# Exponent words one slot pair earlier and a later value-rest copy, in a fused attention and mixture-of-experts kernel on one Trainium2 core

## Chip, cores and metric

The kernel runs on one core of a Trainium2 chip. The metric is device time in microseconds (us) of one execution; three timed runs of the kernel before gave 1537.13, 1540.23 and 1555.36 us, median 1540.23 us. Engines are named as the profile names them: PE is TensorE (PEld its weight loads), DVE is VectorE, ACT is ScalarE, POOL is GpSimd, SP is SyncE, which issues most DMAs.

## What is computed

The reference is pooled-key attention, a dense two-layer block with a leaky ReLU, and a top-1 mixture of eight experts:

```python
k_p = k.reshape(B, H, Sp, 8, D).mean(axis=3)          # B=8, H=8, S=576, D=64, Sp=72
v_p = v.reshape(B, H, Sp, 8, D).mean(axis=3)
attn = softmax(q @ k_p.T / sqrt(D))
x = (attn @ v_p).transpose(0, 2, 1, 3).reshape(4608, 512)
h = x @ w_in                                           # 512 x 2048, float64 in HBM
y = np.maximum(0.01 * h, h) @ w_out                    # 2048 x 512, float64 in HBM
e = argmax(y @ w_gate); g = softmax(y @ w_gate)[e]     # 8 experts
out = g * (np.maximum(y @ w1[e], 0) @ w2[e])           # 512 x 1024 x 512, float64 in HBM
```

The three weight matrices and the activations are multiplied as pairs of float32 parts (high and rest), three products for each.

## The kernel before

**Slots.** The 4608 tokens are 18 blocks of 256 tokens. For each block the dense layer runs over 16 slices f of the 2048 hidden units. One step (block b, slice f) is a slot. Slots 0 to 3 are (0, 0) to (0, 3). From slot 4 to slot 26 the first two blocks alternate: even slots are (0, f), odd slots (1, f - 4). An even slot and the odd one behind it are called a pair here. Slots 27 to 31 finish block 1, and from slot 32 on the blocks follow each other, 16 slots each. The order is written out by hand: each engine gets its instructions in the order in which the loop (the list `seq`, and `at(slot, function)` for work hung on a slot) records them, and works them off in that order.

**What a slot does.** `g1` (L498) makes 12 matmuls of 256 columns into a PSUM bank. ACT copies 0.01 of it (L131, `g<-h`), DVE takes the maximum (L506, `g<-g,h`), ACT rounds it to the high part (L131, `ghl<-g`, function `g_hi`), and in the next slot DVE subtracts that from it for the rest (L134, `ghl<-g,ghl`, function `g_lo`). `g2` (L526) makes 6 matmuls of 512 columns of the slot two before. Two PSUM banks take turns for `g1`.

**Weight conversion.** In slots 0 to 25 the two dense weights of a slice, 128 x 1024 float64 numbers in all, are turned into float32 pairs. `w_load64` (L450, L451) loads both halves into one of three buffers `raw`. `w_conv1a` first lets ACT make the exponent words (L463, absolute value of the top 16 bits into `ab_t`; L464, a Relu with scale and bias that shifts and rebiases into `e_t`), then lets DVE put in the sign (L465, on `e_t`) and shift the high mantissa (L468). `w_conv1b` puts in the low mantissa bits (L474) and joins exponent and mantissa (L477). `w_conv2` lets ACT round to the high part (L131, `w<-raw`) and DVE subtract (L134, `w<-raw,w`). There is one `e_t` and one `ab_t`. The function `conv` hangs this on the slots: in the even slot of a pair with slice f stand `w_conv2(0, f + 1)` and `w_conv1a(f + 2)`, in the odd slot `w_conv2(1, f + 1)`, `w_load64(f + 4)` and `w_conv1b(f + 2)`; in slots 0 to 3 all of it stands in one slot.

**Keys and values of the second batch.** They are loaded unpooled into the places of later weights and pooled by matmuls with a band matrix: `kvn_k` at slots 6, 8, 10 and 12 (L254), `kvn_v` at slot 14 (L269, then ACT and DVE in turn write `vm`, L275), `kvn_r` at slot 16: a product (L282), a masked copy by DVE into the tile that held the values (L284), and `v_rest` (four ACT copies into `vr` and two DVE subtractions, all through helpers at L131 and L134).

**Further on.** Block 0's routing uses transposes of its output (`y_tr`, slots 31 and 32), a small product (`y_logit`, slot 33), `route_a` (slot 34) and `route_b` and `route_c` (slots 36, 38). From slot 34 on the expert weights are split and stored. `final` makes the step list of the experts out of small tiles at the end of the dense part; behind it come the experts' steps.

Of the kernel before, what the change touches and what calls it, by code (L numbers as in the profile page):

```python
# [21 lines left out]
def kernel(  # L22
# [89 lines left out]
    second = []  # L112

    def sb(shape, dt, tag, bufs=1):
        return (second[0] if tag in ("ps", "kv", "y4", "junk") else pool).tile(shape, dt, name=tag, tag=tag, bufs=bufs)
# [163 lines left out]
    def kvn_r(nb):  # L279
        t = kvn[1]  # L280
        p = pt("att")
        nc.tensor.matmul(p[0:64], rep8.rearrange("p a b -> p (a b)"), t[0:64, 4], start=True, stop=True)  # L282
        f = t[0:64, 0].rearrange("p (h d) -> p h d", h=H)
        nc.vector.scalar_tensor_tensor(  # L284
            out=f, in0=p[0:64].rearrange("p (h d) -> p h d", h=H), scalar=float(POOL),
            in1=mask8.unsqueeze(2).to_broadcast([64, H, D]), op0=ALU.mult, op1=ALU.mult,
        )
        v_rest(nb % 2, f)
# [171 lines left out]
    def w_conv1a(f, kinds=BOTH):  # L460
        _, hw, e, ab = words(f, kinds)
        h = raw[f % 3][:, kinds].bitcast(BF16).rearrange("p k (n t) -> p (k n) t", t=4)[:, :, 3]
        nc.scalar.activation(ab, h, AF.Abs)  # L463
        nc.scalar.activation(e, ab.bitcast(U16), AF.Relu, scale=8.0 * 65536.0, bias=ebias)  # L464
        nc.vector.scalar_tensor_tensor(  # L465
            out=e, in0=hw, scalar=0x80000000, in1=e, op0=ALU.bitwise_and, op1=ALU.bitwise_or
        )
        nc.vector.tensor_scalar(  # L468
            out=hw, in0=hw, scalar1=3, scalar2=0x7FFFF8, op0=ALU.logical_shift_left, op1=ALU.bitwise_and
        )  # L470
# [204 lines left out]

    def final(c):
        V = nc.vector
        n = sb([P, E], F32, "fn")
        ni = sb([P, E], I32, "fni")
# [8 lines left out]
        m, m2 = sb(sq, F32, "g", 2), sb(sq, F32, "g", 2)  # L688
        key, pp, u, r = [sb([P, E], F32, "f" + x) for x in ("k", "q", "u", "w")]
        V.scalar_tensor_tensor(out=key, in0=n, scalar=float(E), in1=rank0, op0=ALU.mult, op1=ALU.add)  # L690
        pre, end = sb([P, E], F32, "fp"), sb([P, E], F32, "fe")
        ft = sb([P, 4], F32, "ft")
        tot, row, tv = ft[:, 0:1], ft[:, 1:2], ft[:, 2:3]
        cv = sb([P, 2], F32, "fcv")
# [33 lines left out]
        ri = sb([P, 1], I32, "fri")  # L728
# [3 lines left out]
    def final_list(cv):  # L732
# [6 lines left out]
        er, ch = etab[0:1], sb([1, NSS], F32, "fch")  # L739
# [273 lines left out]
    def plan():  # L1013
# [95 lines left out]
    with tc.manual_schedule():  # L1109
# [5 lines left out]
        e_t = start.tile([P, 1024], U32, name="e_t")  # L1115
# [35 lines left out]
        att_c(0)  # L1151
        w_conv1a(0, slice(0, 1))
# [5 lines left out]
        w_conv2(0, 0)  # L1158
        w_conv1a(0, slice(1, 2))
# [23 lines left out]
        def conv(s, b, f):  # L1183
# [17 lines left out]
        for s, (b, f) in enumerate(seq):  # L1201
# [171 lines left out]
```

## Time and profile before

| | us |
|---|---|
| timed runs | 1537.13, 1540.23, 1555.36 |
| the profiled execution's own time | 1544.75 |
| its span (first to last instruction) | 1542.8 |
| PE busy | 1471.1 |
| DVE busy | 930.8 |
| ACT busy | 618.3 |
| POOL busy | 336.7 |

The span is what the profile's times count from. Busy time leaves out waits. In a timeline row the numbers are start and duration; the bracket behind a row is the idle time of its engine just before, and what ended it. A wait is put down to the releaser that came last. Matmuls are pipelined and their ends are modelled, so a busy PE is not a PE at its peak.

### The profile page before, as it was taken

The page shows a single profiled execution, that of the slowest core. Times are in us where ns is not written, and L with a number is a line of the kernel's source. Part 1 is how long each engine was busy: PE and PEld are TensorE (multiplying, and loading weights), DVE is VectorE, ACT ScalarE, POOL GpSimd, SP SyncE. Part 2 cuts the span into 40 slices and gives each one's busy share as a digit, 9 for nine tenths or more (in the row PEclk, how much of TensorE's full clock was granted, in tenths as well). Part 3 has the DMA queues.
Part 4 walks back from the last instruction along what each step waited for, and adds up shares of the span by engine and source line. Part 5 has one row for each costly group of instructions (what it writes and reads, how often), then busy time and mean ns, then how long its engine had stood idle before and what let it go on. Part 6 is the DMA issues. An engine that isn't in the chain of part 4 may idle for free. (4 is left out here: it accounts for less than half of the span.)

```text
span 1542.8 us, 25661 instructions
## 1 busy us (share of the span) xinstructions
PE 1471.1 (95%) x9272; PEld 1314.5 (85%) x9272; DVE 930.8 (60%) x2387; ACT 618.3 (40%) x1412; POOL 336.7 (22%) x318
## 2 busy tenths in 40 slices
PE   3688999999999999999999999999999999999998
PEld 3575889899898888899989989988899999988886
DVE  6988768888778878877887977774212112111111
ACT  4565534545444454444444444322222222212222
POOL 4000212232232233223222232111121212111111
PEclk8699999999999999999999999999999999999999
DMA  9533145465544545545645634133611118566160
GB/s 214 149 121 117 60 139 166 157 207 174 158 168 166 182 146 187 179 146 167 192 168 154 209 137 164 62 138 138 266 55 48 49 35 324 200 251 261 42 256 19
DMA packets 121385, 238.05 MB, mean 154 GB/s; under 512 B 56845, under 2 KB 65041, under 8 KB 117544
## 3 DMA queue, kind: packets, MB, share of 16 engines
q1 hardware_dynamic: 90312, 139.81, 29.0%
q10 hardware_dynamic: 23328, 76.56, 13.4%
q0 software_dynamic: 7616, 20.01, 3.9%
q8 instruction: 75, 1.23, 0.3%
q14 instruction: 54, 0.44, 0.1%
HBM read 317.78 MB, written 87.38 MB: 263 GB/s over the span
## 5 line engine op out<-in xcount | busy, mean ns | idle before, releaser
L526 PE MATMUL y<-w,ghl 128*128 128x512 f32 x1728 | 466.5, 406 | 3.9 <-DVE ghl L134 3.1
L526 PEld LDWEIGHTS y<-w,ghl 128*128 128x128 f32 x1728 | 309.0, 191 | 64.1 <-DVE ghl L134 9.5
L134 POOL TENSOR_TENSOR ps<-ps 128x512 f32<-128x512 f32 x128 | 181.6, 1418 | 466.1 <-ACT ps L131 395.1
L498 PEld LDWEIGHTS h<-x_t,w 128*128 128x128 f32 x1776 | 238.9, 194 | 36.3 <-DVE w L134 14.7
L498 PE MATMUL h<-x_t,w 128*128 128x256 f32 x1776 | 246.3, 288 | 19.9 <-DVE w L134 12.8
L546 DVE CUSTOM_DVE_ANT_0 junk<-y,wg 128x512 bf16<-128x512 f32 x256 | 201.9, 789 | 1.9
L498 PEld LDWEIGHTS y<-x_t,w 128*128 128x128 f32 x1488 | 193.2, 189 | 9.6
L498 PE MATMUL y<-x_t,w 128*128 128x256 f32 x1488 | 196.2, 282 | 0.0
L938 PE MATMUL y<-w,ghl 128*128 128x512 f32 x672 | 175.4, 399 | 0.9 <-DVE ghl L926 0.9
L938 PEld LDWEIGHTS y<-w,ghl 128*128 128x128 f32 x672 | 119.7, 189 | 22.3 <-DVE ghl L926 1.3
L994 POOL DMA_INDIRECT out_dram<-kv,sidx x40 | 40.2, 1006 | 372.7 <-ACT kv L993 188.0
L131 ACT ACTIVATE g<-h 128x256 f32<-128x256 f32 x164 | 62.8, 383 | 141.3 <-PE h L498 129.1
L926 DVE SCALAR_TENSOR_TENSOR ghl<-h,ghl 128x256 fp32r<-128x256 f32 x56 | 23.8, 425 | 136.1 <-ACT ghl L925 136.1
L506 DVE TENSOR_TENSOR h<-g,h 128x256 f32<-128x256 f32 x132 | 56.0, 425 | 74.3 <-ACT g L131 73.9
L134 DVE TENSOR_TENSOR at_t<-a,at_t 128x512 fp32r<-128x512 f32 x62 | 42.7, 689 | 87.1 <-ACT at_t L131 86.8
L131 ACT ACTIVATE ps<-ps 128x512 fp32r<-128x512 f32 x128 | 80.5, 629 | 20.1 <-DMA ps<-in_moe_w_dram 13.1
L131 ACT ACTIVATE ghl<-h 128x256 fp32r<-128x256 f32 x132 | 50.5, 382 | 91.6 <-PE y L526 43.1
L131 ACT ACTIVATE ghl<-y 128x256 fp32r<-128x256 f32 x124 | 47.2, 380 | 95.2 <-DVE y L506 52.0
L131 ACT ACTIVATE g<-y 128x256 f32<-128x256 f32 x124 | 47.3, 382 | 61.0 <-PE y L498 54.2
L613 POOL DMA_INDIRECT lst<-ent,six x36 | 37.4, 1039 | 152.7 <-DVE six L612 112.7
L297 DVE TENSOR_TENSOR kv<-kv 72x512 f32<-72x512 f32 (+8 forms) x126 | 68.5, 544 | 3.2
L134 DVE TENSOR_TENSOR ghl<-h,ghl 128x256 fp32r<-128x256 f32 x132 | 55.5, 421 | 24.3 <-ACT ghl L131 23.9
(272 smaller groups left out, 2131.3 us busy)
## 6 DMA issues: line engine op xcount, KB each, us to landing
w<-wsp SPq DMA_DIRECT2D x108, 2048.0 KB
wsp<-ps ACTq DMA_DIRECT2D x128, 512.0 KB
ps<-in_moe_w_dram SPq DMA_DIRECT2D x128, 256.0 KB
y_d<-y ACTq DMA_DIRECT2D x18, 512.0 KB
raw<-in_moe_w_in_dram SPq DMA_DIRECT2D x16, 512.0 KB
raw<-in_moe_w_out_dram SPq DMA_DIRECT2D x16, 512.0 KB
q<-in_q_dram SPq DMA_DIRECT2D x28, 256.0 KB
kv<-in_k_dram SPq DMA_DIRECT2D x24, 288.0 KB
```

The lines of the kernel that those rows point to most:

```text
L131: nc.scalar.activation(o, i, AF.Copy, scale=scale)
L134: eng.tensor_tensor(out=o, in0=a, in1=b, op=ALU.subtract)
L297: eng.tensor_tensor(out=o, in0=t[:, :, 0:w], in1=t[:, :, w:2 * w], op=ALU.add)
L498: nc.tensor.matmul(p[:, 0:BLK], win(f)[:, kk, l], xv[:, kk, r], start=(n == 0), stop=(n == 3 * KD - 1))
L506: nc.vector.tensor_tensor(out=g, in0=t, in1=h, op=ALU.max)
L526: nc.tensor.matmul(y_ps[b, i], hl[:, l, i * P:i * P + P], wout(f)[:, r], start=(f == 0 and l + r == 0), stop=(last and l == 1),)
L546: nc.vector.tensor_tensor_reduce(out=jk, in0=y_sb[b][:, i], in1=wg_t[0][:, e], scale=1.0, scalar=0.0, op0=ALU.mult, op1=ALU.add, accum_out ...
L613: nc.gpsimd.indirect_dma_start(out=lst, out_offset=bass.IndirectOffsetOnAxis(ap=ix[:, 0:1], axis=0), in_=ent[:, i, :], in_offset=None, bou ...
L926: nc.vector.scalar_tensor_tensor(out=hl[:, 1], in0=b, scalar=0.0, in1=f32(hl[:, 0]), op0=ALU.max, op1=ALU.subtract)
L938: nc.tensor.matmul(o_ps[2 * p + i], hl[:, l, i * P:i * P + P], w[:, r], start=(f == 0 and l + r == 0), stop=(f == 7 and l == 1),)
L994: nc.gpsimd.indirect_dma_start(out=out, out_offset=bass.IndirectOffsetOnAxis(ap=sidx[:, t:t + 1], axis=0), in_=o, in_offset=None, bounds_c ...
```

## The change

`w_conv1a` loses its two ACT instructions to a new function `w_exp`. There are two exponent tiles, used in turn. `w_exp` of a slice is issued at the end of the odd slot's conversion (behind `w_conv1b(f + 2)`, for slice f + 3); in slots 0 to 3 likewise, and for slices 1 and 2 before slot 0. `v_rest` of the second batch leaves `kvn_r` (slot 16) and is hung on slot 18. Small tiles of the routing move to a pool that is opened after slot 31, block 0's routing is hung on later slots, and `final` takes its scratch from the gate weights' tile.

```diff
+    THIRD = ("junk", "rtmp", "roh", "cnt", "ent", "etmp", "rmx", "six", "erow", "eri")
...
-        return (second[0] if tag in ("ps", "kv", "y4", "junk") else pool).tile(shape, dt, name=tag, tag=tag, bufs=bufs)
+        return (second[0] if tag in ("ps", "kv", "y4") else second[1] if tag in THIRD else pool).tile(shape, dt, name=tag, tag=tag, bufs=bufs)
...
@@ kvn_r
-        v_rest(nb % 2, f)
...
@@ words
-        return rw[:, :, 0], rw[:, :, 1], e_t[:, 0:n], ab_t[:, 0:n]
+        return rw[:, :, 0], rw[:, :, 1], e_t[f % 2][:, 0:n], ab_t[:, 0:n]
...
-    def w_conv1a(f, kinds=BOTH):
-        _, hw, e, ab = words(f, kinds)
+    def w_exp(f, kinds=BOTH):
+        _, _, e, ab = words(f, kinds)
         h = raw[f % 3][:, kinds].bitcast(BF16).rearrange("p k (n t) -> p (k n) t", t=4)[:, :, 3]
         nc.scalar.activation(ab, h, AF.Abs)
         nc.scalar.activation(e, ab.bitcast(U16), AF.Relu, scale=8.0 * 65536.0, bias=ebias)
+
+    def w_conv1a(f, kinds=BOTH):
+        _, hw, e, _ = words(f, kinds)
         nc.vector.scalar_tensor_tensor(
...
@@ final: every sb(...) tile becomes spare(...), a slice of the gate weights' tile
-        n = sb([P, E], F32, "fn")
-        ni = sb([P, E], I32, "fni")
+        n = spare([P, E])
+        ni = spare([P, E], I32)
...
@@ plan, block 0
                 at(30, y_evac, 0)
-                at(31, y_tr, 0, 0)
-                at(32, y_tr, 0, 1)
-                at(33, y_logit, 0)
-                r = (34, 36)
+                at(33, y_tr, 0, 0)
+                at(35, y_tr, 0, 1)
+                at(36, y_logit, 0)
+                r = (37, 39)
...
-        e_t = start.tile([P, 1024], U32, name="e_t")
+        e_t = [start.tile([P, 1024], U32, name=f"e{i}") for i in range(2)]
...
@@ before slot 0
+        w_exp(0, slice(0, 1))
         w_conv1a(0, slice(0, 1))
...
+        w_exp(0, slice(1, 2))
         w_conv1a(0, slice(1, 2))
...
+        w_exp(1)
         w_conv1a(1)
         w_conv1b(1)
+        w_exp(2)
...
         at(16, kvn_r, 1)
+        at(18, v_rest, 1, kvn[1][0:64, 0].rearrange("p (h d) -> p h d", h=H))
...
@@ conv
                 if alone or b == 1:
                     w_conv1b(f + 2)
+                    if f + 3 < NF:
+                        w_exp(f + 3)
...
@@ after slot 31
                 stack.close()
+                second.append(ctx.enter_context(tc.tile_pool(name="third", bufs=1, side="right")))
```

On ACT, one pair of slots before the change (slots 8 and 9; `w_551` and `w_554` are places of converted weights, `raw_112` is the slice whose exponent words are made, `kT` belongs to `kvn_k`):

```order
L131 ACTIVATE w_551<-raw_111 128x4x128
L463 ACTIVATE ab_t<-raw_112 128x1024
L464 ACTIVATE e_t<-ab_t,ebias 128x1024
L131 ACTIVATE ghl<-g 128x256
L131 ACTIVATE g<-h_765 128x256
L131 ACTIVATE w_554<-raw_111 128x512
L131 ACTIVATE ghl<-g 128x256
L131 ACTIVATE g<-h_796 128x256
L131 ACTIVATE kT_71<-a_813 64x72 x2
L131 ACTIVATE w_827<-raw_112 128x4x128
```

The exponent words stand in the even slot, between that slot's rounding of `w_551` and its `ghl<-g`. The same pair after the change:

```order
L132 ACTIVATE w_554<-raw_112 128x4x128
L132 ACTIVATE ghl<-g 128x256
L132 ACTIVATE g<-h_766 128x256
L132 ACTIVATE w_557<-raw_112 128x512
L463 ACTIVATE ab_t<-raw_111 128x1024
L464 ACTIVATE e_109<-ab_t,ebias 128x1024
L132 ACTIVATE ghl<-g 128x256
L132 ACTIVATE g<-h_799 128x256
L132 ACTIVATE kT_71<-a_816 64x72 x2
L132 ACTIVATE w_830<-raw_113 128x4x128
```

They have moved into the odd slot, ahead of that slot's `ghl<-g` and of the next even slot's `g<-h`, and they are of the slice after the one that DVE has in hand.

On DVE, slot 16 before the change (`w_342` is the tile with the second batch's values, `vr_75` their rest):

```order
L506 TENSOR_TENSOR g<-g,h_1009 128x256
L134 TENSOR_TENSOR ghl<-g,ghl 128x256
L284 SCALAR_TENSOR_TENSOR w_342<-a_1026,mask_79 64x512
L134 TENSOR_TENSOR vr_75<-w_342,vr_75 32x256 x2
L134 TENSOR_TENSOR w_827<-raw_112,w_827 128x4x128
L465 SCALAR_TENSOR_TENSOR e_t<-raw_110,e_t 128x1024
```

And DVE in slot 18 after it, where the two `vr` subtractions now stand, ahead of the softmax of a token tile (`st`, `pr`) that stood there already:

```order
L509 TENSOR_TENSOR g<-g,h_1086 128x256
L135 TENSOR_TENSOR ghl<-g,ghl 128x256
L135 TENSOR_TENSOR vr_75<-w_343,vr_75 32x256 x2
L386 TENSOR_REDUCE st<-a_1111 128x4
L135 TENSOR_TENSOR pr<-a_1111,st 128x288
L386 TENSOR_REDUCE st<-a_1118 128x4
L135 TENSOR_TENSOR pr<-a_1118,st 128x288
L135 TENSOR_TENSOR w_1131<-raw_111,w_1131 128x4x128
L468 SCALAR_TENSOR_TENSOR e_108<-raw_112,e_108 128x1024
```

Between the masked copy L284 and these subtractions there are now the rest of slot 16 and all of slot 17.

## Rows read from the trace of the kernel before

**Rows 1.** The page, parts 1 and 2: busy time, and 40 slices of 38.6 us

```profile
PE 1471.1 (95%) x9272; PEld 1314.5 (85%) x9272; DVE 930.8 (60%) x2387; ACT 618.3 (40%) x1412; POOL 336.7 (22%) x318
...
PE   3688999999999999999999999999999999999998
```

**Rows 2.** Windows: length, busy (instructions) by engine, granted clock, DMA share, GB/s

```profile
80.00:180.00 100.00, 88.65 (x520) 72.89 (x521) 83.68 (x142) 58.99 (x111) 10.29 (x26) 0.97 0.31 93
180.00:200.00 20.00, 20.00 (x141) 18.44 (x140) 6.19 (x14) 8.45 (x19) 0.00 (x0) 1.00 0.41 153
81.80:90.39 8.59, 8.59 (x57) 7.79 (x56) 6.91 (x10) 5.25 (x11) 0.00 (x0) 1.00 0.42 130
```

**Rows 3.** What DVE waited for, 36 to 175 us: us, times, longest

```profile
DVE e_t L465 <- ACT e_t L464: 12.1, 11, 1.5
DVE vr L134 <- ACT vr L131: 1.4, 2, 0.9
DVE w L134 <- ACT w L131: 1.1, 2, 0.9
```

**Rows 4.** Timeline of slots 6 to 8: start, us, engine, line, operation, [idle before]

```profile
82.98 1.58 PE L498 MATMUL h<-x_t,w 128*128 128x256 f32 x12
...
87.34 0.41 DVE L506 TENSOR_TENSOR g<-g,h 128x256 f32<-128x256 f32 x1
...
88.04 1.13 ACT L463 ACTIVATE ab_t<-raw 128x1024 bf16<-128x1024 bf16 x1
...
89.21 1.15 ACT L464 ACTIVATE e_t<-ab_t,ebias 128x1024 uint32<-128x1024 uint16 x1
...
89.90 1.59 PE L498 MATMUL h<-x_t,w 128*128 128x256 f32 x12
90.26 0.40 ACT L131 ACTIVATE ghl<-g 128x256 fp32r<-128x256 f32 x1
90.39 1.23 DVE L465 SCALAR_TENSOR_TENSOR e_t<-raw,e_t 128x1024 uint32<-128x1024 uint32 x1 [1.53 <-ACT e_t L464]
90.69 0.39 ACT L131 ACTIVATE g<-h 128x256 f32<-128x256 f32 x1
...
93.64 0.34 SPq L451 DMA_DIRECT2D raw<-in_moe_w_out_dram  x1
...
95.93 0.41 DVE L506 TENSOR_TENSOR g<-g,h 128x256 f32<-128x256 f32 x1
96.05 0.67 ACT L131 ACTIVATE w<-raw 128x512 fp32r<-128x512 f32 x1 [2.19 <-DVE raw L477]
...
96.75 0.69 DVE L134 TENSOR_TENSOR w<-raw,w 128x512 fp32r<-128x512 f32 x1
...
98.96 1.22 DVE L465 SCALAR_TENSOR_TENSOR e_t<-raw,e_t 128x1024 uint32<-128x1024 uint32 x1 [1.51 <-ACT e_t L464]
```

**Rows 5.** Timeline, before slot 0: the first slice's exponent words

```profile
39.10 1.23 DVE L465 SCALAR_TENSOR_TENSOR e_t<-raw,e_t 128x1024 uint32<-128x1024 uint32 x1 [1.21 <-ACT e_t L464]
```

**Rows 6.** Timeline, slot 16: the rest of the values

```profile
132.99 1.71 ACT L131 ACTIVATE vr<-w 32x256 fp32r<-32x256 f32 x4 [3.79 <-DVE w L284]
133.43 0.42 DVE L134 TENSOR_TENSOR vr<-w,vr 32x256 fp32r<-32x256 f32 x1 [0.48 <-ACT vr L131]
...
134.73 0.41 DVE L134 TENSOR_TENSOR vr<-w,vr 32x256 fp32r<-32x256 f32 x1 [0.88 <-ACT vr L131]
...
136.02 0.69 DVE L134 TENSOR_TENSOR w<-raw,w 128x512 fp32r<-128x512 f32 x1 [0.88 <-ACT w L131]
```

**Rows 7.** Timeline, slot 14: the value product on PE, and DVE's first subtraction

```profile
116.02 3.65 PE L269 MATMUL a<-w,band 128*64 128x512 f32 x8
...
122.33 0.41 DVE L275 SCALAR_TENSOR_TENSOR vm<-a,vm 64x256 fp32r<-64x256 f32 x1
```

**Rows 8.** A window of 0.5 us behind the load issued at 93.64, columns as rows 2

```profile
97.00:97.50 0.50, 0.50 (x4) 0.40 (x3) 0.45 (x1) 0.50 (x1) 0.00 (x0) 1.00 0.00 0
```

**Rows 9.** Timeline, slots 35 and 36: PE waits for DVE behind the routing

```profile
209.70 1.69 PE L498 MATMUL h<-x_t,w 128*128 128x256 f32 x12 [0.78 <-DVE ghl L134]
```

More of the change, by code (lines that the diff above doesn't have):

```diff
@@ L674, in early, with spare @@
         return fetch(ri[0:NE, 0:1], NE, 0)
+    spare_at = [0]
+    def spare(shape, dt=F32):
+        n = shape[1] * (shape[2] if len(shape) > 2 else 1)
+        o = wg_t[0].rearrange("p e d -> p (e d)")[0:shape[0], spare_at[0]:spare_at[0] + n]
+        spare_at[0] += n
+        if dt != F32:
+            o = o.bitcast(dt)
+        return o if len(shape) == 2 else o.rearrange("p (a b) -> p a b", b=shape[2])
     def final(c):
         V = nc.vector
-        n = sb([P, E], F32, "fn")
-        ni = sb([P, E], I32, "fni")
+        n = spare([P, E])
+        ni = spare([P, E], I32)
         V.tensor_scalar(out=ni, in0=c[:, 0], scalar1=float(P - 1), scalar2=None, op0=ALU.add)
@@ L687, in final @@
         T, isp, thr, ng, du, c5 = [stepc[:, i:i + 1] for i in range(6)]
-        m, m2 = sb(sq, F32, "g", 2), sb(sq, F32, "g", 2)
-        key, pp, u, r = [sb([P, E], F32, "f" + x) for x in ("k", "q", "u", "w")]
+        m, m2 = spare(sq), spare(sq)
+        key, pp, u, r = [spare([P, E]) for _ in range(4)]
         V.scalar_tensor_tensor(out=key, in0=n, scalar=float(E), in1=rank0, op0=ALU.mult, op1=ALU.add)
-        pre, end = sb([P, E], F32, "fp"), sb([P, E], F32, "fe")
-        ft = sb([P, 4], F32, "ft")
+        pre, end = spare([P, E]), spare([P, E])
+        ft = spare([P, 4])
         tot, row, tv = ft[:, 0:1], ft[:, 1:2], ft[:, 2:3]
-        cv = sb([P, 2], F32, "fcv")
+        cv = spare([P, 2])
         V.tensor_copy(ni, n)
@@ L712, in final @@
         V.tensor_tensor(out=end, in0=pre, in1=r, op=ALU.add)
-        sel = sb([P, E], F32, "fd")
-        s2 = sb([P, E], F32, "fr")
+        sel = spare([P, E])
+        s2 = spare([P, E])
         V.tensor_scalar(out=sel, in0=pre, scalar1=T, scalar2=cv[:, 1:2], op0=ALU.is_le, op1=ALU.mult)
         V.tensor_scalar(out=s2, in0=end, scalar1=T, scalar2=None, op0=ALU.is_gt)
-        base = sb([P, E], F32, "fb")
+        base = spare([P, E])
         V.tensor_scalar(out=u, in0=u, scalar1=du, scalar2=None, op0=ALU.mult)
@@ L727, in final @@
         V.tensor_reduce(row, base, axis=AX.X, op=ALU.add)
-        ri = sb([P, 1], I32, "fri")
+        ri = spare([P, 1], I32)
         V.scalar_tensor_tensor(out=ri, in0=row, scalar=float(E * CAP), in1=tv, op0=ALU.add, op1=ALU.add)
@@ L738, in final_list @@
             )
-        er, ch = etab[0:1], sb([1, NSS], F32, "fch")
+        er, ch = etab[0:1], spare([1, NSS])
         V.tensor_copy(er[:, 2:2 + NPS], p[0:1, 0:2 * NPS:2])
```

## Prediction

> **What bounds the kernel now.** I read the page first. PE is busy for 95% of the span, and its slices of 38.6 us fall below nine tenths only in the first four, up to 154 us, and in the last [rows 1]. So the early stalls are what can be saved. The windows say where. From 180 us on PE has no idle time: 20.00 of 20 us, with 18.44 us of weight loads. From 80 to 180 us it is busy for 88.65 of 100 us and loads weights for only 72.89, while DVE is busy for 83.68 [rows 2]. That is the stretch in which pairs of slots are worked and weights converted.
>
> The list of waits of DVE tells what it lacks there. The top row is L465, the first conversion step of DVE, behind L464, ACT's exponent words: 12.1 us in 11 waits. Far below stand the two `vr` subtractions (1.4 us) and the `w` subtraction (1.1 us) [rows 3]. The timeline shows the ring. At 90.39 DVE starts L465. Its work of one pair ends with the `w` subtraction, at 96.75 + 0.69 = 97.44. Then it stands until 98.96, when the next L465 starts [rows 4]: 7.05 us of work, 1.52 us of waiting, 8.57 us for a pair. ACT could not be quicker: its copy `w<-raw` waited 2.19 us for DVE's L477, began at 96.05, took 0.67, and behind it come the two exponent instructions, 1.13 and 1.15 us long [rows 4]. DVE in that time has only a maximum, a subtraction and a `w` subtraction to do. So DVE sets the pace of a pair, and ACT's two instructions stand in its ring.
>
> PE is not in that ring. Between 82.98 and 89.90 it ran one pair, pooling of keys included, with nothing to wait for but its own work: 6.92 us [rows 4]. That it shows 8.59 of 8.59 us busy in the first such window [rows 2] is because it was still catching up.
>
> **Exponent words one pair earlier.** No instruction is added or removed; the two ACT instructions go from the even slot to the odd one, for the next slice, into the other buffer. L465 then finds its words made some 7 us before. What goes is the wait: 12.1 us less the first, 1.21 us [rows 5], which stays because slice 1's words still stand right before L465 there. That is 10.9 us. What is late next for L465 is DVE itself, so a pair should take 7.05 us, just above PE's 6.92.
>
> I check that the moved instructions are hidden on ACT. Behind the odd slot's `g<-h` now come `w<-raw`, the two, `ghl<-g` and the even slot's `g<-h`: 0.67 + 1.13 + 1.15 + 0.40 + 0.39 = 3.74 us. DVE needs that last copy for its even maximum. From its odd maximum to that one it has 0.41 for the maximum, about as much for the subtraction, 0.69 for the `w` subtraction, and for L474 and L477, of L465's size, 1.23 each: 3.97 us. The odd `g<-h` is early too: it ended at 91.08, in front of a DVE that was busy with L465 until 91.62 and has L468 to do after that [rows 4]. So ACT keeps up; its work for a pair is 5.25 us [rows 2]. If that cover were gone, each of ten odd slots would give up to 2.28 us back.
>
> The moved instructions also wait for something new: the load of slice f + 3, one slot earlier than before. The second half of a load is issued when DVE's odd `w` subtraction is done, here at 93.64 [rows 4], and by 97.00 no byte moves any more [rows 8]: 3.4 us. From that issue to the even maximum that needs the copies behind the words it is L474, L477 and a whole pair, 2.4 + 7.05 = 9.5 us, and the words with the two copies behind them take 1.13 + 1.15 + 0.40 + 0.39 = 3.1 us. So the load may take 6.4 us; it has 3.0 to spare. I take 0 for this wait; the ends are 0 and, where loads queue behind the unpooled values in slots 0 to 3, 1.5 us once.
>
> **The value rest in slot 18.** The four ACT copies (1.71 us) and the two subtractions remain. In slot 16 the copies waited 3.79 us for the masked copy L284 and DVE waited for them in turn: 0.48 + 0.88, and 0.88 for the `w` subtraction queued behind [rows 6]: 2.24 us. In slot 18 their input is a slot old, and ACT can run them while DVE is in L474 and L477; I take all 2.2 us as saved. The subtractions' 0.83 us are moved, not saved. The end on the other side is that half the waits come back with the softmax beside them, 1.1 us. PE gains nothing of its own, since it too follows DVE there.
>
> **What is late next.** At slot 14 DVE so far comes late: PE starts the value product at 116.02, is done 3.65 later, ACT's copy takes some 0.4, so its result is there at 120.1, and DVE reaches its subtraction at 122.33 [rows 7]. Without the waits at L465 from 81.80 to 116.13, 6.6 of the 12.1 us, it would be there at 115.7. PE, at 6.92 us a pair from 82.98, starts slot 14 at 110.7, ends the matmuls of that slot 1.6 later and the product at 115.9, and ACT's copy at 116.3. So DVE waits 0.6 us: a new loss.
>
> **Routing and scratch.** The transposes and the small product of block 0 move by two or three slots, with the same instructions. PE waited 0.78 us for DVE near them [rows 9]; it may lose that wait or meet another one like it, and I take 0 between -0.8 and +0.8. The scratch of `final` keeps its order and its instructions, so 0.
>
> **The sum.** 10.9 + 2.2 - 0.6 = 12.5 us. Behind slot 26 PE has no idle time [rows 2], and the slots set all later work, so what DVE gains up to its last conversion reaches the end. The profiled execution took 1544.75 us, 1.95 more than its span; it would take 1532.2. It ran 4.5 us over the median, so against the median of 1540.23 the forecast is 1527.7 us.
>
> **Two rules.** By matmul busy, PE's room from 80 to 180 us is 11.35 us [rows 2]; my sum has about 11.7 us in that stretch, so it would not quite fit. The Trainium skill's page "Perfetto Trace Analysis", section "Identifying the Most-Contended Engine", says that matmul busy time is a poor measure of the room and weight loads a better one. By weight loads the stretch needs 72.89 x 20 / 18.44 = 79 us, a room of 21. By busy time the forecast would be 1528.1, by the rule it stays; the pair of 6.92 us in 8.57 sides with the rule.
>
> The Trainium skill's page "TensorE: Matmul & The Clock Gate", section "Architectural detail: the array is 16× 32×32, not 1× 128×128", says that ACT's queue is strictly first in, first out. It speaks against putting 2.28 us of words ahead of copies that others wait for. The trace agrees: `ghl<-g` began at 90.26, behind the words, although DVE's maximum, its input, was done at 87.75 [rows 4]. The last rival is what that would cost.
>
> **Rivals.**
> - *PE takes over.* DVE at 7.05 and PE at 6.92 us are close, and PE's second products wait for DVE's subtractions. If they get in step badly, a pair takes perhaps 7.6, and eight pairs give back 8 x 0.55 = 4.4 us: 1532.1. For it: DVE's load is then near 100%. Against: PE runs up to two slots ahead. Chance 0.17.
> - *New waits on ACT.* The loads of slots 0 to 3 and the first pairs land late, or the rest of the values waits as before: 1.5 + 1.1 us once and 0.5 in eight pairs, 6.6 in all: 1534.3. Chance 0.10.
> - *The gain is lost later,* in a stretch set by transfers: 1540. Against it stands PE without idle time from 180 us on. Chance 0.07.
> - *Slower.* The words wait for the load in ACT's queue, and `ghl<-g` and `g<-h` with them. From a landing of 6.4 us on, each further microsecond lengthens the pair. At 8.7, 2.28 more than may be, the pair is 7.05 + 2.28 = 9.33, 0.76 over today's; ten of them cost 7.6: 1547.8. For it: the megabyte of a pair now has to come in 7.05 us. Against: 3.4 us of landing, and DMA engines busy for 0.42 of such a window [rows 2]. Chance 0.05.
>
> **Numbers.** The forecast has 0.61, with a range of its own from 1523 to 1532. The timed runs differ by 3.1 us without the highest. The low end takes all the waits of rows 3 (14.6), 0.8 from the routing and that spread: 1540.23 - 15.4 - 3.1 = 1521; I give 1520. The high end takes in the first two rivals with the spread: 1537. No case reaches 2% (30.8 us), which is about what a measurement of this kernel tells from no change: faster 0.01, same 0.98, slower 0.01.
>
> **What would show it.** Right: the row of L465 behind L464 falls from 12.1 us to about 1.2; L465 follows L465 after 7.0 to 7.3 us between slots 6 and 12; the last L477 starts near 157 us instead of 169.30; the `vr` waits are gone; PE's weight loads from 80 to 180 us rise. Wrong: waits of `g<-g,h` for ACT's `g<-h` over 3 us in the pairs, waits of L463 for loads, pairs over 7.6 us, or an early stretch that is 12 us shorter while the end is not.

## The result, and the profile after

The changed kernel takes 1531.03 us (median of 4 runs, 1525.26 to 1533.83); the kernel before, run beside it, 1542.74 (4 runs). The ratio is 0.9897, 95% interval 0.9862 to 0.9933 (the two medians alone give 0.9924, inside it): some 1% faster, less than the 2% that counted as a change. The profiled execution took 1533.83 us, 10.9 us less than that of before; its span is 1532.1 us, 10.7 less.

The code has moved: L464 is still the Relu of the exponent words, but L465 is now L468, L468 is L471, L474 is L477, the join L477 is L480, `g1` L501, the maximum L509, `g2` L529, the helpers L132 and L135, `vm` L276.

The page's parts 1 and 2 of the changed kernel (40 slices of 38.3 us):

```profile
PE 1468.8 (96%) x9272; PEld 1315.8 (86%) x9272; DVE 929.5 (61%) x2387; ACT 619.1 (40%) x1412; POOL 337.5 (22%) x318
...
PE   4698999999999999999999999999999999999998
```

PE does the same instructions in nearly the same time; its slices one and three are a tenth fuller [rows 1]. Windows of the same kernel (length, busy time of PE, PEld, DVE, ACT, POOL, granted clock, DMA share, GB/s); the second is one pair:

```profile
80.00:180.00 100.00, 95.75 (x608) 83.04 (x607) 86.89 (x151) 62.02 (x121) 10.29 (x26) 0.98 0.35 108
...
87.32:94.29 6.97, 6.97 (x49) 6.42 (x48) 6.82 (x11) 5.14 (x10) 0.00 (x0) 1.00 0.48 150
```

Between 80 and 180 us PE now loads weights for 83.04 us instead of 72.89 [rows 2]; so much more of its work has come forward into this stretch. A pair takes 6.97 us instead of 8.57. All that DVE waits for between 36 and 175 us:

```profile
DVE g L509 <- ACT g L132: 5.9, 4, 2.0
DVE vm L276 <- ACT vm L132: 1.4, 2, 1.0
DVE e L468 <- ACT e L464: 1.2, 1, 1.2
DVE w L135 <- ACT w L132: 0.3, 1, 0.3
```

The row of 12.1 us in 11 waits [rows 3] has become one wait of 1.2; the `vr` row is gone. The 5.9 us at L509 stand at 164.48 and later, behind the last join at 156.48, where the copies that L509 waits for wait for PE's matmuls in turn. The timeline of one pair (start, us, engine, line, operation, [idle before]), to be laid beside [rows 4]:

```profile
87.32 1.22 DVE L468 SCALAR_TENSOR_TENSOR e<-raw,e 128x1024 uint32<-128x1024 uint32 x1
...
88.73 1.14 ACT L463 ACTIVATE ab_t<-raw 128x1024 bf16<-128x1024 bf16 x1
...
89.91 1.15 ACT L464 ACTIVATE e<-ab_t,ebias 128x1024 uint32<-128x1024 uint16 x1
...
90.56 0.34 SPq L451 DMA_DIRECT2D raw<-in_moe_w_out_dram  x1
90.97 0.40 ACT L132 ACTIVATE ghl<-g 128x256 fp32r<-128x256 f32 x1
91.27 0.36 ACT L132 ACTIVATE g<-h 128x256 f32<-128x256 f32 x1
...
91.71 1.23 DVE L480 TENSOR_TENSOR raw<-raw,e 128x1024 uint32<-128x1024 uint32 x1
...
92.85 0.42 DVE L509 TENSOR_TENSOR g<-g,h 128x256 f32<-128x256 f32 x1
92.97 0.68 ACT L132 ACTIVATE w<-raw 128x512 fp32r<-128x512 f32 x1 [0.74 <-DVE raw L480]
...
94.29 1.22 DVE L468 SCALAR_TENSOR_TENSOR e<-raw,e 128x1024 uint32<-128x1024 uint32 x1
```

None of these DVE rows has a bracket any more. ACT makes the words from 88.73 to 91.06 while DVE converts the slice before them, and its `g<-h` is done at 91.63, well ahead of the maximum at 92.85 that needs it. The words are read by the sign step at 94.29, so they are ready 3.2 us before their use: they moved by one slot, half a pair.

### The profile page after: what moved, and what is told of

The parts are those of the page before. It is cut to its first block, busy times and chain, and to the rows that moved or that the text cites. A ratio compares the mean times of both kernels' runs of the same rounds, so it can differ in the third digit from the quotient of the medians.

```text
span 1532.1 us, 25665 instructions
## 1 busy us (share of the span) xinstructions
PE 1468.8 (96%) x9272; PEld 1315.8 (86%) x9272; DVE 929.5 (61%) x2387; ACT 619.1 (40%) x1412; POOL 337.5 (22%) x318
## 5 line engine op out<-in xcount | busy, mean ns | idle before, releaser
L529 PE MATMUL y<-w,ghl 128*128 128x512 f32 x1728 | 464.4, 406 | 0.9 <-DVE spf L781 0.6
L529 PEld LDWEIGHTS y<-w,ghl 128*128 128x128 f32 x1728 | 309.7, 191 | 58.5 <-DVE ghl L135 3.1
L135 POOL TENSOR_TENSOR ps<-ps 128x512 f32<-128x512 f32 x128 | 181.8, 1421 | 473.6 <-ACT ps L132 391.2
L501 PEld LDWEIGHTS h<-x_t,w 128*128 128x128 f32 x1776 | 236.0, 192 | 32.3 <-DVE w L135 13.6
L501 PE MATMUL h<-x_t,w 128*128 128x256 f32 x1776 | 242.7, 286 | 16.4 <-DVE w L135 12.2
L501 PEld LDWEIGHTS y<-x_t,w 128*128 128x128 f32 x1488 | 193.2, 189 | 9.6
L501 PE MATMUL y<-x_t,w 128*128 128x256 f32 x1488 | 196.2, 282 | 0.0
L132 ACT ACTIVATE g<-h 128x256 f32<-128x256 f32 x164 | 62.8, 383 | 151.7 <-PE h L501 140.9
L939 DVE SCALAR_TENSOR_TENSOR ghl<-h,ghl 128x256 fp32r<-128x256 f32 x56 | 23.8, 425 | 136.0 <-ACT ghl L938 136.0
L509 DVE TENSOR_TENSOR h<-g,h 128x256 f32<-128x256 f32 x132 | 56.0, 424 | 77.1 <-ACT g L132 76.4
L135 DVE TENSOR_TENSOR at_t<-a,at_t 128x512 fp32r<-128x512 f32 x62 | 42.7, 688 | 86.9 <-ACT at_t L132 86.4
L132 ACT ACTIVATE ghl<-h 128x256 fp32r<-128x256 f32 x132 | 50.7, 384 | 94.3 <-PE y L529 47.0
L132 ACT ACTIVATE ps<-ps 128x512 fp32r<-128x512 f32 x128 | 80.4, 628 | 15.5 <-DMA ps<-in_moe_w_dram 9.8
L132 ACT ACTIVATE ghl<-y 128x256 fp32r<-128x256 f32 x124 | 47.3, 382 | 94.1 <-DVE y L509 50.6
L132 ACT ACTIVATE g<-y 128x256 f32<-128x256 f32 x124 | 47.4, 382 | 61.4 <-PE y L501 53.8
L135 DVE TENSOR_TENSOR ghl<-h,ghl 128x256 fp32r<-128x256 f32 x132 | 55.5, 420 | 24.8 <-ACT ghl L132 24.5
```

The source lines that it names most:

```text
L132: nc.scalar.activation(o, i, AF.Copy, scale=scale)
L135: eng.tensor_tensor(out=o, in0=a, in1=b, op=ALU.subtract)
L501: nc.tensor.matmul(p[:, 0:BLK], win(f)[:, kk, l], xv[:, kk, r], start=(n == 0), stop=(n == 3 * KD - 1))
L509: nc.vector.tensor_tensor(out=g, in0=t, in1=h, op=ALU.max)
L529: nc.tensor.matmul(y_ps[b, i], hl[:, l, i * P:i * P + P], wout(f)[:, r], start=(f == 0 and l + r == 0), stop=(last and l == 1),)
L939: nc.vector.scalar_tensor_tensor(out=hl[:, 1], in0=b, scalar=0.0, in1=f32(hl[:, 0]), op0=ALU.max, op1=ALU.subtract)
```

## Experiments

"Pair" is the distance from one sign step (L468) to the next in slots 6 to 12; "last join" the start of the last L480; "mark" the issue of the gate weights' load at the end of slot 31, where the interleaved part of blocks 0 and 1 is over. These rows give the last two, for the changed kernel (timeline of DVE and of SP):

```profile
156.48 1.23 DVE L480 TENSOR_TENSOR raw<-raw,e 128x1024 uint32<-128x1024 uint32 x1
...
176.34 0.32 SPq L1246 DMA_DIRECT2D wg<-wgT_d  x1
```

and this the mark of the kernel before, whose last join started at 169.30:

```profile
188.62 0.32 SPq L1225 DMA_DIRECT2D wg<-wgT_d  x1
```

All in us; the ratio is to the kernel before, run beside the kernel of that row (the medians of before were 1542.74, 1543.40, 1545.13 and 1547.20 us on these occasions). pe_less, dve_less and both_less leave out part of the computation and ran once each; their whole times decide nothing.

| kernel | median (runs) | ratio, 95% | pair | last join | mark |
|---|---|---|---|---|---|
| before | 1542.74 (4) | | 8.57 | 169.30 | 188.62 |
| changed | 1531.03 (4) | 0.9897, 0.9862–0.9933 | 6.97 | 156.48 | 176.34 |
| words_alone | 1531.47 (6) | 0.9931, 0.9899–0.9962 | 6.96 | 158.82 | 178.68 |
| rest_alone | 1539.71 (10) | 0.9987, 0.9962–1.0011 | 8.56 | 166.88 | 186.27 |
| one_buffer | 1561.95 (4) | 1.0140, 1.0098–1.0183 | 9.10 | 185.65 | 207.09 |
| words_twice | 1535.39 (10) | 0.9947, 0.9924–0.9969 | 7.5 | 160.52 | 180.39 |
| routing_back | 1531.82 (7) | 0.9910, 0.9883–0.9937 | 6.97 | 156.20 | 176.06 |
| words_even | 1538.87 (10) | 0.9961, 0.9935–0.9988 | 8.0–8.3 | 161.37 | 181.22 |
| pool_sub | 1534.18 (9) | 0.9923, 0.9900–0.9947 | 7.2–7.4 | 160.86 | 180.20 |
| pool_both | 1534.43 (6) | 0.9922, 0.9894–0.9950 | 7.2–7.6 | 159.53 | 178.88 |
| pe_less | 1526.63 (1) | | 6.96 | 155.84 | 173.74 |
| dve_less | 1529.08 (1) | | 6.94 | 152.13 | 172.53 |
| both_less | 1521.66 (1) | | 6.43 | 149.34 | 167.79 |
| early_first | 1529.40 (10) | 0.9912, 0.9887–0.9936 | 6.97 | 155.12 | 174.97 |

Runs of one kernel differ by several us (see the last section), so the early marks decide, not the whole times. All diffs are against the changed kernel.

**The two parts, each alone.** words_alone puts the value rest back into slot 16:

```diff
@@ kvn_r
+        v_rest(nb % 2, f)
@@ before slot 0
-        at(18, v_rest, 1, kvn[1][0:64, 0].rearrange("p (h d) -> p h d", h=H))
```

> The changed kernel with the value rest back in slot 16; the exponent words stay one pair ahead. Theory (the words carry 10.9 us, the rest 2.2): pairs of slots 6 to 12 stay at about 7.0 us; the waits for vr and w in slot 16 come back with 2.2 us, and the last join of exponent and mantissa, which starts at 169.30 us before and at 156.48 after, starts near 158.7 us; the time is some 10 us under before, 2 us over after. Rival (the stall of slot 16 hides behind something else once the words are early): the last join starts at 156.5 to 157 us as after, and no time is lost. Rival (the two parts need each other): over 162 us.

rest_alone makes the exponent words right before the sign step again:

```diff
-        w_exp(2)
@@ conv
+                    w_exp(f + 2)
                     w_conv1a(f + 2)
...
-                    if f + 3 < NF:
-                        w_exp(f + 3)
```

> The changed kernel with the exponent words issued directly in front of their use, as before; the value rest stays in slot 18. Theory: the list of waits shows the first conversion step behind the words with about 12 us again, pairs of slots 6 to 12 take 8.57 us, the last join starts near 167 us (169.30 less 2.2), and the time is about 2 us under before, no difference that can be measured. Rival (PE's lead decides and not the words): pairs under 8 us and a last join before 163 us.

DVE's waits, 36 to 175 us, of words_alone and then of rest_alone:

```profile
DVE vr L135 <- ACT vr L132: 1.4, 2, 0.9
DVE e L469 <- ACT e L465: 1.2, 1, 1.2
DVE w L135 <- ACT w L132: 1.2, 2, 0.9
```

```profile
DVE e L468 <- ACT e L464: 11.6, 11, 1.6
```

In both lists the rows of just one part come back. The last join comes 10.5 us earlier by the words and 2.4 by the rest, 12.9 together; with both it is 12.8. The parts add up (traces of single executions; the first sign step stands at 39.10 to 39.35 us in these four, so 0.2 us more or less means nothing). By whole time the rest alone can't be told from nothing.

**The second buffer.**

```diff
-        e_t = [start.tile([P, 1024], U32, name=f"e{i}") for i in range(2)]
+        e_t = [start.tile([P, 1024], U32, name="e0")] * 2
```

> The changed kernel with one exponent tile in place of two; all instructions keep their order. Theory: the second exponent instruction must then wait for the join of the slice before, the last step of DVE in an odd slot, and behind it in ACT's order stand the high part and the even slot's copy: 1.15 + 0.40 + 0.39 = 1.9 us in which DVE waits, so pairs of 8.9 us in place of 6.97, a last join at 175 us or later, and a time 3 to 13 us over before. Rival (the order alone makes the gain, since the words are issued behind the join anyway): as after, pairs of 7.0 us and a last join near 156.5 us.

It was slower than before, by 1.4%, and by more than I expected. Timeline rows of one_buffer in a pair:

```profile
97.70 1.15 ACT L464 ACTIVATE e<-ab_t,ebias 128x1024 uint32<-128x1024 uint16 x1 [3.08 <-DVE raw L480]
...
99.46 0.42 DVE L509 TENSOR_TENSOR g<-g,h 128x256 f32<-128x256 f32 x1 [1.85 <-ACT g L132]
```

With one tile, L464 may write only when DVE's join has read the words of the slice before. ACT stands there for 3.08 us with `ghl<-g` and `g<-h` queued behind it, and DVE then waits 1.85 us for `g<-h`. This is the last rival's mechanism, with the buffer in the place of the load; over 36 to 175 us it makes 23.8 us of waits at L509. The pair of 9.10 is near the 8.9 expected. The time is 18.6 us over before and not 3 to 13, since slots 0 to 3 lose 2 to 3 us each too, which the expected text does not count. The earlier issue pays only together with the second tile; the second tile without it, in rest_alone, changes nothing in the pair (8.56).

**Room on ACT.** words_twice makes each slice's words a second time in the odd slots:

```diff
                     if f + 3 < NF:
                         w_exp(f + 3)
+                        if not alone:
+                            w_exp(f + 3)
```

> The changed kernel with the two exponent instructions issued twice in each odd slot from slot 5 on (the second time to the same result), 2.28 us more of ACT for a pair. Theory (ACT has about 1.8 us to spare for a pair): ACT's work for a pair goes from about 5.3 to 7.5 us and it becomes the pace; pairs of slots 6 to 12 take 7.6 to 8.2 us, DVE waits for the copy of the matmul result, the last join starts at 163 to 169 us, and the time lies 6 to 12 us over after. Rival (PE sets the pace at 6.92 us and ACT has more room): pairs under 7.2 us.

The pair grew by 0.53 us, to 7.5, less than the 7.6 to 8.2 expected, and the last join (160.52) and the time (some 4 us over the changed kernel) stayed under their ranges too. In one such pair ACT was busy for 7.36 of 7.52 us: twice the words fill ACT, and it sets the pace. So ACT has room for all but about 0.5 us of another pair of instructions.

**Where the words stand.** words_even issues the same words in the even slot, behind the sign step:

```diff
                     w_conv1a(f + 2)
+                    if not alone and f + 3 < NF:
+                        w_exp(f + 3)
...
-                    if f + 3 < NF:
+                    if f + 3 < NF and alone:
                         w_exp(f + 3)
```

> The changed kernel with the exponent words, still one pair ahead and in two buffers, issued half a pair earlier: at the end of the even slot's conversion. Theory (a load takes 3.4 us from its issue, which the odd slot's second subtraction sets, and ACT works in order): the words now wait for the load in most pairs, the list of ACT's waits shows the first exponent instruction behind the load with 0.2 to 0.7 us each, and the even slot's high part and the odd slot's copy come behind them; DVE waits for that copy, pairs of slots 6 to 12 take 7.4 to 8.2 us, and the last join starts at 160 to 167 us. Rival (any slot a pair ahead will do): pairs of 7.0 us, last join near 156.5 us.

ACT's waits for loads in words_even, 36 to 175 us (in the changed kernel 0.2 us in one wait):

```profile
ACT ab_t L463 <- DMA raw<-in_moe_w_out_dram: 4.3, 8, 0.9
```

The load lands up to 0.9 us late, ACT's queue stands, and the pair is 8.0 to 8.3 us. But the load is only half of it. In the three pairs from 87.61 on, the words wait 0.48, 0.52 and 0.72 us, and the pairs are 1.06, 1.09 and 1.30 us longer than 6.97: always some 0.6 us more than the wait. That remainder fits ACT's order. Between the even and the odd maximum ACT now has `w<-raw`, the two words, `ghl<-g` and `g<-h`, 3.8 us in sum, and DVE only 3.4 us (maximum, two subtractions, L468 and L471). Half a pair later the load is in time, and DVE has L477 and L480 there, 4.0 us in sum with its maximum and two subtractions. Two thirds or more of the gain of 1.6 us a pair hang on the odd slot.

**Relieving DVE by POOL.** pool_sub gives the subtraction of the second weight of each slice to POOL; pool_both also the first weight's in slots 0 to 3:

```diff
@@ w_conv2, pool_sub
-        sub(nc.vector, dl, w, f32(dh))
+        sub(nc.gpsimd if kind == 1 else nc.vector, dl, w, f32(dh))
```

> The changed kernel with the subtraction of the second weight (odd slots, and slots 0 to 3) on POOL instead of DVE: 0.69 us less of DVE for a slice. Theory (DVE at 6.97 and PE at 6.92 us a pair are both at their limit): pairs of slots 6 to 12 stay at 6.9 us, now set by PE; slots 0 to 3 and the pairs from slot 16 on, where DVE has more to do, gain 0.5 to 0.7 us each, and the last join starts at 150 to 153 us; time some 4 us under after. Rival (DVE alone sets the pace): pairs of 6.3 us, last join near 147 us. Rival (POOL's subtraction, 1.42 us where it stands for the expert weights, slows DVE beside it or delays the loads): last join at 156 us or later.

> As the run with the second subtraction on POOL, and in slots 0 to 3 the first one too. Theory (in slots 0 to 3 DVE is full, and PE waits for the first subtraction, which stands behind the softmax steps in DVE's order): another 0.7 us less of DVE in each of four slots, PE's wait for that subtraction gets shorter, and the last join starts 2 to 3 us earlier than in that run; time 2 us less. Rival (POOL's 1.42 us makes the first subtraction later than DVE's, and PE waits longer): last join no earlier.

DVE has 16 instructions less, 11 us, and yet the pairs grew to 7.2 to 7.4 us and the last join came 4.4 us later: the last rival of the first text. DVE's groups, 36 to 170 us (count, busy us, mean ns, idle before), in the changed kernel:

```profile
L135 DVE TENSOR_TENSOR ghl<-g,ghl 128x256 fp32r<-128x256 f32 x28 | 11.7, 419 | 0.0
L471 DVE TENSOR_SCALAR raw<-raw 128x1024 uint32<-128x1024 uint32 x15 | 10.4, 696 | 0.5
```

and in pool_sub:

```profile
L471 DVE TENSOR_SCALAR raw<-raw 128x1024 uint32<-128x1024 uint32 x15 | 15.7, 1044 | 1.7 <-DVE e L468 0.5
L135 DVE TENSOR_TENSOR ghl<-g,ghl 128x256 fp32r<-128x256 f32 x27 | 13.6, 504 | 0.0
```

Two rows of pool_sub's timeline show why:

```profile
97.68 1.36 POOL L135 TENSOR_TENSOR w<-raw,w 128x512 fp32r<-128x512 f32 x1 [5.09 <-ACT w L132]
...
97.95 1.64 DVE L471 TENSOR_SCALAR raw<-raw 128x1024 uint32<-128x1024 uint32 x1
```

L471 alone gives 5.3 us back, `ghl` 2.3 more (27 times 85 ns). In all six places where L471 began inside POOL's subtraction it took 1.27 to 1.64 us instead of 0.70, and ended 0.55 us behind POOL's end (here 99.59 and 99.04). Where it began first, at 90.72, it took 0.70, and POOL's subtraction, from 90.75, 1.84. The Trainium skill's page "SBUF — State Buffer", section "Who interferes with whom", says that VectorE and GpSimd share one pair of ports, held by one instruction at a time from start to end, and names tensor_scalar among those that can take it. These rows agree in that L471 ends only behind POOL's instruction, but by 0.55 us and not by its full 0.70. With the other groups (last section) the slower instructions took back more than the 11 us. From 36 us to the last join DVE is busy for 118.7 us in pool_sub, in the changed kernel for 115.2. In pool_both the last join is 1.3 us earlier than in pool_sub, not 2 to 3, L471 is slower still (1209 ns on average), and the whole time is the same.

**Who sets the pair now.** In the window 87.32 to 94.29 PE is busy throughout and none of DVE's instructions waits (6.82 of 6.97 us busy). pe_less drops 2 of 12 matmuls of `g1` in blocks 0 and 1, dve_less halves the sign step, both_less does both:

```diff
@@ g1, pe_less
+        parts = [(kk, l, r) for kk in range(KD) for l, r in ((0, 0), (0, 1), (1, 0))]
+        if b < 2:
+            parts = [t for t in parts if t[0] < 2 or t[1] == 0]
@@ w_conv1a, dve_less
+        m = 512 if f > 1 else e.shape[1]
         nc.vector.scalar_tensor_tensor(
-            out=e, in0=hw, scalar=0x80000000, in1=e, op0=ALU.bitwise_and, op1=ALU.bitwise_or
+            out=e[:, 0:m], in0=hw[:, 0:m], scalar=0x80000000, in1=e[:, 0:m], op0=ALU.bitwise_and, op1=ALU.bitwise_or
```

> Question: in a pair of slots of 6.97 us neither PE nor DVE has idle time; which of them sets it? The changed kernel with 10 instead of 12 matmuls in g1 of blocks 0 and 1: left out are the products of the weight rests with the activations' high parts for half of the contraction. PE has 4 x 0.133 = 0.53 us less per pair, DVE and ACT the same. DVE sets the pair: L468 still follows L468 after 6.95 to 7.0 us in slots 6 to 12, PE shows idle time of some 0.4 us per pair, the last join stays between 156 and 157. PE sets it: 6.4 to 6.8 us per pair, the last join near 153. Whole time: behind the conversion PE has 4 matmuls fewer in slots 27 to 31 only, so some 1 to 2 us under the changed kernel by the first, 4 to 5 by the second.

> The changed kernel with the sign put into only half of the exponent words from slice 2 on (L468 on 128x512 instead of 128x1024, 0.69 instead of 1.22 us), so the sign is left out for one of the two weights. DVE has 0.53 us less per pair, PE and ACT the same. DVE alone sets the pair: it falls to 6.45 us. PE alone sets it: it stays at 6.95 to 7.0. The two are level (my theory): it falls by under 0.1 us, to 6.85 to 6.95, which is then PE's own pace, and DVE shows some 0.4 us of waits per pair. The values differ, and with them the routing of tokens, so the whole time says nothing.

> Both cuts together: 10 matmuls in g1 of blocks 0 and 1, and the sign in only half of the exponent words. If PE and DVE are level and nothing else stands close behind them, the pair falls to 6.4 to 6.5 us. If ACT's words, loads or PSUM banks stand close behind, it stays over 6.7 and waits of the maximum for ACT's copy, or of the exponent words for loads, appear. The whole time says nothing, as with the sign cut alone.

The sign steps of pe_less, then of dve_less (timeline of DVE):

```profile
94.71 1.22 DVE L468 SCALAR_TENSOR_TENSOR e<-raw,e 128x1024 uint32<-128x1024 uint32 x1
...
101.67 1.22 DVE L468 SCALAR_TENSOR_TENSOR e<-raw,e 128x1024 uint32<-128x1024 uint32 x1
```

```profile
91.81 0.68 DVE L469 SCALAR_TENSOR_TENSOR e<-raw,e 128x512 uint32<-128x512 uint32 x1
...
98.75 0.69 DVE L469 SCALAR_TENSOR_TENSOR e<-raw,e 128x512 uint32<-128x512 uint32 x1
```

With less on PE the pair stays at 6.96: DVE sets it. With less on DVE it is 6.43 and 6.77 while PE still catches up, then twice 6.94: that is PE's pace. With both cuts it is 6.43 four times. So the two engines are level within 0.03 us, and nothing else stands within half a microsecond behind them. I had expected PE to show 0.4 us of idle time a pair in pe_less; its matmul time shows none in the first two pairs (6.97 of 6.97, 6.96 of 6.96) and 0.16 us in the third, though it had four matmuls less in each. Only the pace tells, not the busy time.

**The moved routing, and the last wait.** routing_back puts block 0's routing on its old slots; early_first does that too and issues slice 1's words before DVE converts the second half of slice 0:

```diff
@@ routing_back and early_first
-                at(33, y_tr, 0, 0)
-                at(35, y_tr, 0, 1)
-                at(36, y_logit, 0)
-                r = (37, 39)
+                at(31, y_tr, 0, 0)
+                at(32, y_tr, 0, 1)
+                at(33, y_logit, 0)
+                r = (34, 36)
@@ early_first
         w_exp(0, slice(1, 2))
+        w_exp(1)
         w_conv1a(0, slice(1, 2))
...
-        w_exp(1)
         w_conv1a(1)
```

> The changed kernel with block 0's routing on its old slots (transposes 31 and 32, product 33, the rest 34, 36 and 38). Theory (the later slots cost about 0.4 us): the issue of the gate weights' load at the end of slot 31 stays at 176.3 us, and the issue of the query load of slot 40, 209.67 us after the change, comes at 209.2 to 209.4; the whole time is no different by measurement. Rival (moving it had removed PE's wait of 0.78 us): the query load comes at 210.0 us or later.

> Two small gains added to the changed kernel: block 0's routing back on its old slots, and the exponent words of slice 1 issued before DVE converts the second half of slice 0, so that the one wait left at L468 (1.20 us at 39.11) goes. If that wait sets the start of the slots, the last join comes 0.8 to 1.2 us earlier (155.0 to 155.7) and the whole time is 1529.5 to 1531. The rival: the words, 2.3 us long, now stand ahead of the copies of x_t on ACT (34.01), which the first slot's matmuls need, so that PE starts up to 1.4 us later; the last join then stays at 156 to 157 and the time at 1531 to 1532. A difference this small is under what 3 rounds tell; the join and the marks decide.

In routing_back the last join, which is ahead of the routing, and the mark are already 0.28 us earlier than in the changed kernel; the load of `q` in slot 40 is 0.53 earlier (209.14 against 209.67) and the next one 0.70 (240.71 against 241.41). So the later routing costs the rest, 0.25 to 0.4 us, in one execution of each; whole times don't show it. In early_first the wait of 1.2 us at L468 is gone, the last join 1.36 us earlier and the later `q` load 1.79 (239.62). Its median of 1529.40 is nominally the lowest of the kernels that do the whole computation, but its interval overlaps that of the changed kernel: better than before for certain, better than the change by the marks alone.

## Why the prediction was right, and where it was off

The forecast was 1527.7 us, range 1520 to 1537, no change by 2%; measured 1531.03. Point by point:

- *Exponent words, 10.9 us.* Right. 12.1 us of waits became 1.2, and the 1.2 stands where it was [rows 5]:

```profile
39.11 1.23 DVE L468 SCALAR_TENSOR_TENSOR e<-raw,e 128x1024 uint32<-128x1024 uint32 x1 [1.20 <-ACT e L464]
```

- *The pair.* 7.05 predicted, 6.97 measured, because the sign step begins 0.08 us before the subtraction ahead of it ends (94.29 against 93.68 + 0.69). The prediction has the words ready some 7 us before their use; it is 3.2 us (91.06 to 94.29), which was still enough. That DVE sets it, just above PE, is shown by pe_less and dve_less; PE's own pace is 6.94, not 6.92.
- *ACT and the load.* Right: no waits of L509 in the pairs. After the load issued at 90.56 no byte moves from 94.00 on (a window of 0.5 us), 3.4 us as in [rows 8]:

```profile
94.00:94.50 0.50, 0.50 (x7) 0.50 (x6) 0.50 (x2) 0.00 (x0) 0.00 (x0) 1.00 0.00 0
```

The words that read it start 1.7 us later (timeline):

```profile
95.68 1.19 ACT L463 ACTIVATE ab_t<-raw 128x1024 bf16<-128x1024 bf16 x1
```

- *The value rest, 2.2 us.* Right: 2.4 at the last join of rest_alone. The four copies stand at 129.05 and the two subtractions run without a wait, unlike [rows 6]:

```profile
129.05 1.70 ACT L132 ACTIVATE vr<-w 32x256 fp32r<-32x256 f32 x4
...
131.32 0.86 DVE L135 TENSOR_TENSOR vr<-w,vr 32x256 fp32r<-32x256 f32 x2
```

- *The new wait at slot 14.* It came, at 0.97 us and not the 0.6 of the sum. PE's product started at 111.38, DVE reached its subtraction at 114.50; the prediction had worked out 112.3 and 115.7 from [rows 7], so PE came 0.9 us earlier and DVE 1.2:

```profile
111.38 3.65 PE L270 MATMUL a<-w,band 128*64 128x512 f32 x8
...
115.06 0.38 ACT L132 ACTIVATE vm<-a 64x256 fp32r<-64x256 f32 x1 [2.58 <-PE a L270]
...
115.47 0.41 DVE L276 SCALAR_TENSOR_TENSOR vm<-a,vm 64x256 fp32r<-64x256 f32 x1 [0.97 <-ACT vm L132]
```

- *Routing, 0 between -0.8 and +0.8.* It costs 0.25 to 0.4; PE's wait of 0.78 us [rows 9] is now 1.2 in two (PE's waits, 174 to 215 us):

```profile
PE h L501 <- DVE ghl L135: 1.2, 2, 0.9
```

The scratch of `final`, which the prediction put at 0, was not tried alone; across the end of the dense part the lead does not shrink (9.6 us at 1039 us of the kernel before, 10.4 or more from 1067 us on).

- *The sum.* 12.5 us predicted; 12.8 at the last join, 12.3 at the mark, 12.0 and 11.9 at the two `q` loads behind the routing. The sum held to 0.3 us up to the mark, in part because small misses cancel: the shorter pairs and the value rest gave more, the wait at slot 14 took 0.4 us more, and the routing then cost some 0.3. (The low end of the range adds up to 1521.7, not 1521.)
- *"What DVE gains up to its last conversion reaches the end."* It reached the dense part whole: by the issues of the `q` loads the lead is 11.9 us at each one from 241 to 368 us (times of the changed kernel). But the profiled executions differ by 10.9 us, not 12.5. The lead was 14.3 us at 402 us, 16.1 at 671, 11.1 at 782 and 9.6 at 892, and 10.7 at the end. The steps up to 892 lie where PE stood and the granted clock then fell, in one of the two executions or for longer in one (last section). The last one lies near 1049 us, where PE in the kernel before waits 0.9 us for a gather (L903) and the changed kernel does not.
- *The anchor.* Of the miss of 3.3 us, 2.5 are the median that I subtracted from: 1540.23 of three runs; a fourth run made it 1542.74, and 13 to 23 runs on other occasions gave 1543.4 to 1547.2. The other 0.8 is the difference of the two medians, 11.7 us, against the sum's 12.5. The median of so few runs, each some us off by chance, was the weakest term.
- *Two rules.* The gain by itself does not tell them apart. Of the 12.3 us up to the mark, 1.4 were won ahead of slot 4; from slot 4's sign step (81.80 before, 80.36 after) to the mark it is 10.8, less than the 11.35 us of room that matmul busy time left. What matmul busy time does in that stretch tells them apart, before and after (columns as above):

```profile
81.80:188.62 106.82, 95.64 (x569) 79.16 (x567) 85.66 (x147) 61.45 (x119) 10.29 (x26) 0.97 0.29 89
```

```profile
80.36:176.34 95.98, 91.73 (x574) 79.06 (x572) 85.08 (x148) 60.94 (x118) 10.29 (x26) 0.98 0.33 99
```

Weight loads stay at 79.1 us, but the matmuls, five more of them by count, are busy for 3.9 us less (by the mean clocks, 0.97 and 0.98, about 1 us of that is the clock, an estimate), and PE is still idle for 4.25 us. So matmul busy time is no fixed need, and room counted from it comes out too small. The Trainium skill's page "Perfetto Trace Analysis", section "Identifying the Most-Contended Engine", says that weight loads are the better measure; these rows agree.
- *Rivals.* PE did not get out of step (no pair over 7.0 us in slots 6 to 12), no new waits of note came on ACT (0.2 us for a load, once), and no transfer took the gain behind the conversion (the lead holds at 11.9 us up to 368 us). The slower rival's mechanism, ACT's queue standing with `ghl<-g` and `g<-h` behind the words, is real: one_buffer and words_even show it, with 9.10 and about 8.1 us a pair. It stayed away because of the second tile and the odd slot.

## What to carry to other kernels

Where two engines work in a ring, look whether the second engine's part needs anything from the ring itself; if its input is there a step earlier, give it its own buffer and issue it a step ahead, in the half of the step in which its load has landed. Work out first what the ring becomes without it and which engine is next: here the gain ended where VectorE met TensorE, within 0.03 us. Check the size of a small gain by the lead at fixed marks of the trace, not by whole times alone.

## What was not expected of the hardware

**POOL's subtraction stops DVE's TENSOR_SCALAR.** 0.70 us alone, up to 1.64 beside it, shown above. Moving 11 us of work to an idle engine cost 12 us elsewhere on DVE: 5.3 at L471, 2.3 at `ghl`, 1.5 at the other `w` subtractions (15 of them at 788 instead of 686 ns), 1.1 at L477 (1292 instead of 1222 ns) and 1.9 at four small TENSOR_SCALAR of the softmax (L397, 128x8, 172 ns each in the changed kernel, up to 939 in pool_sub).

**The clock in the middle of the dense part.** Windows of 5 us of the kernel before, then of the changed one (columns as above; the number behind POOL is the granted clock):

```profile
405.00:410.00 5.00, 3.31 (x30) 3.23 (x28) 3.87 (x9) 2.92 (x7) 1.92 (x2) 0.97 0.33 129
410.00:415.00 5.00, 5.00 (x20) 4.20 (x20) 1.72 (x4) 1.61 (x3) 1.68 (x1) 0.69 0.00 0
```

```profile
765.00:770.00 5.00, 3.34 (x25) 3.05 (x24) 3.88 (x11) 2.48 (x8) 2.51 (x2) 0.98 0.17 52
770.00:775.00 5.00, 5.00 (x25) 5.00 (x25) 2.37 (x6) 1.13 (x3) 0.00 (x0) 0.50 0.26 105
775.00:780.00 5.00, 5.00 (x14) 3.94 (x14) 1.72 (x4) 1.61 (x3) 1.38 (x1) 0.50 0.01 2
```

PE stood for 1.7 us in the first window of each, waiting for the value rest of a later batch (`vr` on DVE, ahead of L439), and then ran at less than full clock: at 0.50, the 1.2 instead of the 2.4 GHz level, for the ten microseconds 770 to 780 of the changed kernel, which is 5 us of work lost; between the `q` loads at 671 and 782 its lead fell by 5.0. The kernel before went through the same step at full clock, though it waited there too. PE's waits at that step, 764 to 781 us of the changed kernel and 779 to 791 us of the one before:

```profile
PE a L439 <- DVE vr L135: 1.7, 1, 1.7
```

```profile
PE a L439 <- DVE vr L134: 1.5, 1, 1.5
```

The kernel before in turn had its own fall at 410. The changed kernel waited at that step too, 1.1 us, and kept its clock; its lead grew by 2.4:

```profile
390.00:395.00 5.00, 3.90 (x28) 3.55 (x28) 3.88 (x11) 2.48 (x8) 2.51 (x2) 1.00 0.15 52
```

Both have such a fall near 890, behind waits of 1.1 and 1.2 us. Near 650 only the kernel before has one, though both wait 2.2 us there, for another tile (`at_t`, ahead of L361). So a wait stands ahead of each of these falls, but its length alone does not decide. In the traces of all 14 kernels the windows of 5 us from 180 to 1060 us with a clock under 0.93 lie at different steps; the time lost in them, 5 us times the missing part of the clock, is 4.5 us in the kernel before, 8.5 in the changed one, 1.4 in early_first and 16.6 in pool_both. So executions differ by several us by this alone. The mean granted clock of the changed kernel's four runs goes along with that, if not in order: 0.982 and 0.981 where it took 1533.83 and 1531.59 us, 0.985 and 0.986 where it took 1530.46 and 1525.26. Where in those runs it fell is not known. What decides whether a stall is followed by a fall stays open, and a kernel without these waits was not tried; the one fall at 770 cost 5 us, nearly half of what the change brought.
